# Computing what tokens read (attention weights times state) on eight array tiles with features on partitions, and loading the first weights first, in a fused attention and feed-forward kernel

## The chip, the cores and the metric

One Trainium2 chip, one of its cores. The metric is device time in microseconds (us) of one execution. A profile is one traced execution, whose span is a little shorter than the time of a run. Engines are named PE (TensorE), PEld (its weight loads), DVE (VectorE), ACT (ScalarE), POOL (GpSimd) and SP (the queue that issues most transfers).

## The reference

Eight batches of 512 tokens and 32 state rows, 8 heads of 64 features. Tokens read from the state, the state reads from the tokens, and each row of the result, normalised by its root mean square, goes through a gated feed-forward. Cut to what matters:

```python
scores = scale * np.matmul(x, state.transpose(0, 1, 3, 2))     # 512 x 32 for a head
a = softmax(scores)
xread = np.matmul(a, state)                                    # what tokens read
sread = np.matmul(softmax(scale * state @ x.T), x)             # what states read
x = concat([xread, sread]) as rows of 8 * 64 = 512 features
rms = np.sqrt(np.mean(x * x, axis=-1, keepdims=True) + 1e-06)
xn = x / rms * rms_g
out = silu(xn @ w_gate) * (xn @ w_val) @ w_out                 # 512 -> 1536 -> 512
```

All three weight matrices come as 64-bit floats. The kernel turns them into float32 itself.

## The kernel before

It never stores what tokens read. The feed-forward's first products are made as `a` times (state times weights), so `xread` is needed only for its sum of squares, from which the inverse root mean square follows. Heads lie on partitions as 4 groups `j` of 32 state rows, for `e` = 0 and 1. The old read multiplies attention weights `aT` by a block-diagonal tile `bd` of the state, tokens on partitions, and lets ACT add up the squares along the free axis:

```python
for j in range(4):                          # POOL fills the block-diagonal tile
    GE.tensor_copy(bd[Ns*j:Ns*j+Ns, :, j, :], packed[Ns*j:Ns*j+Ns])
...
ss = two.tile([P, NC], F32, name="ss")
for c in range(NC):                         # 4 chunks of 128 tokens
    rp = aps.tile([P, 2, 4 * D], F32, name="at")
    for e in range(2):
        TE.matmul(out=rp[:, e, :], lhsT=aT[:, e, c, :],
                  rhs=bd[:, e].rearrange("p j d -> p (j d)"), start=True, stop=True)   # L270
    flat = rp.rearrange("p e f -> p (e f)")
    SE.activation(out=flat, in_=flat, func=ACTF.Square, scale=DM ** -0.5,
                  accum_out=ss[:, c:c + 1])                                          # L273
    yield
rp = inverse_rms(ss, NC)                    # DVE: + 1e-6 (L174), POOL: pow -0.5 (L176),
aT_s[b] = ...                               # PE: 4 transposes (L179), DVE: scale aT (L278)
```

`attention(b + 1)` is a generator: its steps are interleaved with the feed-forward of batch b, two after each pair of hidden slices and five at each of four places of the output products. The order in which each engine's instructions stand in the trace isn't quite the source's: products are moved into gaps when the program is made (in one steady batch of the kernel before, output products run from 225.63 to 233.86 us between two groups of the read's). Batches 1 to 7 use a scheme with seven products in place of eight; its output part begins:

```python
zs = ...; product(zs, S_, TS(0), True)      # S_ = hs, sums of hidden halves, made on DVE
p5 = keep(zs)
... s = s - hb[upper] (DVE)
xs = ...; product(xs, A(0, 0), B(0, 0), True)   # needs hb alone
p1 = keep(xs)
between()                                   # five steps of attention(b + 1)
```

Weights come in 18 pieces of 1 MB. A piece is loaded raw, then ACT and DVE work on it in eight steps; the last multiplication is on DVE for the first twelve pieces and on POOL for the last six, those of `w_out`. The start is:

```python
load_x(0, nc.scalar)
load_state(0)                               # 4 small transfers
load_piece(0)
nc.sync.dma_start(out=rms_g, ...)
for k in range(1, RAW_AHEAD): load_piece(k)
for _ in attention(0): pass                 # nothing else for PE to do yet
```

Of the kernel before, what the change touches and what calls it, by code (L numbers as in the profile page):

```python
# [8 lines left out]
F32 = mybir.dt.float32  # L9
I32 = mybir.dt.int32  # L10
U32 = mybir.dt.uint32
ALU = mybir.AluOpType
ACTF = mybir.ActivationFunctionType
AXX = mybir.AxisListType.X
PSUM = bass.MemoryType.PSUM

P = 128
# [4 lines left out]
def kernel(  # L22
# [19 lines left out]
    nc = tc.nc  # L42
    VE, SE, GE, TE = nc.vector, nc.scalar, nc.gpsimd, nc.tensor

    B, H, S, D = x.shape
    Ns = state.shape[2]
    DM = H * D
    DFF = moe_w_gate.shape[1]
    NC = S // P
    NI = DM // P  # L50
    NM = DFF // P
# [5 lines left out]
    consts = ctx.enter_context(tc.tile_pool(name="consts", bufs=1))  # L57
    one = ctx.enter_context(tc.tile_pool(name="one", bufs=1))
    two = ctx.enter_context(tc.tile_pool(name="two", bufs=2))
    aps = ctx.enter_context(tc.tile_pool(name="aps", bufs=2, space=PSUM))  # L60
    vps = ctx.enter_context(tc.tile_pool(name="vps", bufs=2, space=PSUM))
# [6 lines left out]
    conv = early.enter_context(tc.tile_pool(name="conv", bufs=2))  # L68


    bds = [consts.tile([P, 2, 4, D], F32, name="bd%d" % r) for r in range(2)]
    for t in bds:
        GE.memset(t, 0.0)
    rows = {}
    x_sb = {}

    def load_state(b):

        rows[b] = two.tile([P, 2, D], F32, name="rows")
        for j in range(4):  # L80
            src = state[b, 2 * j:2 * j + 2].rearrange("e n d -> n e d")
            nc.sync.dma_start(out=rows[b][Ns * j:Ns * j + Ns], in_=src)

    def load_x(b, queue):
        x_sb[b] = one.tile([P, NC, H * D], F32, name="x_b")
        for c in range(NC):
            queue.dma_start(
                out=x_sb[b][:, c].rearrange("p (h d) -> p h d", h=H),
                in_=x[b, :, P * c:P * c + P, :].rearrange("h p d -> p h d"))
# [5 lines left out]
    ones = consts.tile([P, P], F32, name="ones")  # L95
    GE.memset(ones, 1.0)
    bounds = consts.tile([P, 2], F32, name="bounds")
# [10 lines left out]
    pieces = []  # L108
# [7 lines left out]
    raw = {}  # L116

    def load_piece(k):
        if k >= len(pieces):
            return  # L120
        dst, src = pieces[k]
        if src.dtype == F32:
            src = src.rearrange("p a (c f) -> p a c f", f=P)
            for a in range(src.shape[1]):
                nc.sync.dma_start(out=dst[:, a], in_=src[:, a])
            return
        raw[k] = raws.tile([P, 8 * P, 2], I32, name="raw")
        nc.sync.dma_start(out=raw[k].rearrange("p (a f) two -> p a (f two)", a=src.shape[1]),
                          in_=src.bitcast(I32))

    n_ready = 0

# [7 lines left out]
    def to_float32(k):  # L140


        load_piece(k + RAW_AHEAD)
        if k not in raw:
            return
        r = raw.pop(k)
        hi = r[:, :, 1]
        man = r.bitcast(F32)[:, :, 0]
        top = conv.tile([P, 8 * P], I32, name="top")
        ex = conv.tile([P, 8 * P], I32, name="ex")  # L150
        VE.tensor_scalar(ex, hi, 20, 0x7ff, op0=ALU.logical_shift_right, op1=ALU.bitwise_and)

        SE.activation(out=ex, in_=ex, func=ACTF.Relu, scale=-1.0, bias=bounds[:, 0:1])
        SE.activation(out=ex, in_=ex, func=ACTF.Relu, scale=-float(1 << 23), bias=bounds[:, 1:2])
        SE.activation(out=man, in_=r.bitcast(U32)[:, :, 0], func=ACTF.Copy, scale=2.0 ** -52)
        VE.tensor_scalar(top, hi, 0xfffff, 0x100000, op0=ALU.bitwise_and, op1=ALU.bitwise_or)
        VE.scalar_tensor_tensor(out=man, in0=top, scalar=2.0 ** -20, in1=man,
                                op0=ALU.mult, op1=ALU.add)
        VE.scalar_tensor_tensor(out=ex, in0=hi, scalar=-(1 << 31), in1=ex,
                                op0=ALU.bitwise_and, op1=ALU.bitwise_or)  # L160
        dst = pieces[k][0]
        eng = VE if k < NM else GE
        eng.tensor_tensor(out=dst, in0=man.rearrange("p (a c f) -> p a c f", f=P, c=dst.shape[2]),  # L163
                          in1=ex.bitcast(F32).rearrange("p (a c f) -> p a c f", f=P,
                                                        c=dst.shape[2]), op=ALU.mult)


    stT_g = {}
# [2 lines left out]

    def inverse_rms(ss, n):

        VE.tensor_scalar(ss, ss, 1e-6, None, op0=ALU.add)  # L174
        ri = two.tile([P, NC], F32, name="ri")
        GE.tensor_tensor(out=ri[:, 0:n], in0=ss, in1=mhalf[:, 0:n], op=ALU.pow)  # L176
        rp = aps.tile([P, NC, P], F32, name="at")
        for c in range(n):
            TE.transpose(out=rp[:, c, :], in_=ri[:, c:c + 1].to_broadcast([P, P]), identity=ident)  # L179
        return rp.rearrange("p c t -> p (c t)")  # L180

    def attention(b):
        xb, packed, bd = x_sb.pop(b), rows.pop(b), bds[b % 2]
        if b + 1 < B:
            load_state(b + 1)

# [3 lines left out]
        TE.transpose(out=tp.rearrange("p j n -> p (j n)"),  # L190
                     in_=packed.rearrange("p e d -> p (e d)"), identity=ident)
        VE.tensor_copy(stT, tp)
        for j in range(4):
            GE.tensor_copy(bd[Ns * j:Ns * j + Ns, :, j, :], packed[Ns * j:Ns * j + Ns])
        VE.tensor_tensor(out=stT_g[b], in0=stT, in1=rms_g.unsqueeze(2).to_broadcast([P, 4, Ns]),
                         op=ALU.mult)
        yield
# [10 lines left out]
        sp = [aps.tile([P, S], F32, name="at") for e in range(2)]  # L208
        for j in range(4):
            for e in range(2):  # L210
                TE.matmul(out=sp[e][Ns * j:Ns * j + Ns, :], lhsT=stT[D * e:D * e + D, j, :],  # L211
                          rhs=xT[j // 2][D * e:D * e + D, j % 2].rearrange("p c t -> p (c t)"),
                          start=True, stop=True)
        sS = one.tile([P, 2, NC, P], F32, name="sS", tag="sS")
        e2 = one.tile([P, 2, NC, P], F32, name="e2", tag="xT0")
        s2 = two.tile([P, 2], F32, name="s2")
        m2 = two.tile([P, 2], F32, name="m2")
        z2 = two.tile([P, 2], F32, name="z2")
        for e in range(2):
            SE.copy(sS[:, e].rearrange("p c t -> p (c t)"), sp[e])  # L220
            VE.reduce_max(out=m2[:, e:e + 1], in_=sS[:, e].rearrange("p c t -> p (c t)"),  # L221
                          axis=AXX)
        yield

        eS = one.tile([P, NC, 2, 4, Ns], F32, name="eS", tag="eS")
# [2 lines left out]
        for cp in range(2):  # L228
            tp = aps.tile([P, 2, 2, P], F32, name="at")
            for c in range(2):  # L230
                for e in range(2):
                    TE.transpose(out=tp[:, c, e, :], in_=sS[:, e, 2 * cp + c, :], identity=ident)
            srows = tp.rearrange("p c e (j n) -> p (c e j) n", n=Ns)
            a = eS[:, 2 * cp:2 * cp + 2].rearrange("p c e j n -> p (c e j) n")
# [3 lines left out]
                             op=ALU.subtract)  # L238
            SE.activation(out=a, in_=a, func=ACTF.Exp, scale=SCALE)
            yield  # L240

        VE.tensor_scalar(s2, m2, -SCALE, None, op0=ALU.mult)
        for e in range(2):
            SE.activation(out=e2[:, e], in_=sS[:, e], func=ACTF.Exp, scale=SCALE,  # L244
                          bias=s2[:, e:e + 1], accum_out=z2[:, e:e + 1])
        yield
        aT = one.tile([P, 2, NC, P], F32, name="aT", tag="sS")
        for cp in range(2):
            a = eS[:, 2 * cp:2 * cp + 2].rearrange("p c e j n -> p (c e j) n")
# [5 lines left out]
                             op=ALU.mult)  # L255
            tp = aps.tile([P, 2, 2, P], F32, name="at")
            for c in range(2):
                for e in range(2):
                    TE.transpose(out=tp[:, c, e, :],
                                 in_=eS[:, 2 * cp + c, e].rearrange("p j n -> p (j n)"),  # L260
# [2 lines left out]
            yield  # L263


        ss = two.tile([P, NC], F32, name="ss")
        for c in range(NC):
            rp = aps.tile([P, 2, 4 * D], F32, name="at")
            for e in range(2):
                TE.matmul(out=rp[:, e, :], lhsT=aT[:, e, c, :],  # L270
                          rhs=bd[:, e].rearrange("p j d -> p (j d)"), start=True, stop=True)
            flat = rp.rearrange("p e f -> p (e f)")
            SE.activation(out=flat, in_=flat, func=ACTF.Square, scale=DM ** -0.5,  # L273
                          accum_out=ss[:, c:c + 1])
            yield
        rp = inverse_rms(ss, NC)
        aT_s[b] = two.tile([P, 2, S], F32, name="aT_s")
        VE.tensor_tensor(out=aT_s[b], in0=aT.rearrange("p e c t -> p e (c t)"),  # L278
# [33 lines left out]
    def state_norm():  # L312

        sq = one.tile([P, NI, NT], F32, name="sqT", tag="eS")
        SE.activation(out=sq, in_=xsT, func=ACTF.Square, scale=DM ** -0.5)
        sp = aps.tile([P, NT // P], F32, name="at")
        for r in range(NT // P):
            for i in range(NI):
                TE.matmul(out=sp[:, r:r + 1], lhsT=sq[:, i, P * r:P * r + P], rhs=ones[:, 0:1],
                          start=(i == 0), stop=(i == NI - 1))  # L320
        ss = two.tile([P, NT // P], F32, name="sst")
        VE.tensor_copy(ss, sp)
        rp = inverse_rms(ss, NT // P)
        for i in range(NI):
            VE.scalar_tensor_tensor(out=xsT[:, i, :], in0=xsT[:, i, :], scalar=rms_g[:, i:i + 1],
                                    in1=rp[:, 0:NT], op0=ALU.mult, op1=ALU.mult)
        yield
# [238 lines left out]
    done = object()  # L566
    sums = iter(())
    load_x(0, nc.scalar)
    load_state(0)
    load_piece(0)  # L570
    nc.sync.dma_start(out=rms_g, in_=moe_rms_g.rearrange("(i p) -> p i", p=P))
    for k in range(1, RAW_AHEAD):
        load_piece(k)
# [79 lines left out]
```

## Time and profile before

| | before |
|---|---|
| time, median of 3 | 888.15 us (887.88 to 888.86) |
| span of the profile | 887.1 us |
| PE, DVE, ACT, POOL busy | 94, 52, 39, 21% |
| first product of the seven-product scheme | 172.5 us |
| PE idle after 199 us | 13.8 of 688 us |

The slices of the page show a head (to about 155 us), where PE often waits for DVE (12.4 us in two waits for `eS`), and a long part where PE is full. I use two marks throughout. The first is the **first product of seven**, the start of batch 1's feed-forward (batches 1 to 7 use a scheme with seven products in place of eight): from there on PE is full (busy 22.00 of the 22 us to 199 us), so the mark tells how long the head took. The second is the **period**, from that product of one batch to that of the next.

### The profile page before, as it was taken

To read this page: it belongs to the slowest core of one execution; us is meant where nothing else is said; L and a number is where in the kernel's file an instruction comes from. 1 tells how busy PE (TensorE), PEld (TensorE's weight loads), DVE (VectorE), ACT (ScalarE), POOL (GpSimd) and SP (SyncE) were. 2 spreads that over 40 slices of the span, in tenths; PEclk is the share of its full clock that TensorE was granted. 3 is DMA by queue.
4 is the path that set the end of the run, shared out by engine and by line. 5 is a ranking of instruction groups with operands and counts; after the bars stand their busy time and mean duration, and the time that the engine had idled before them with its cause. 6 is when DMAs were issued, how large, how long until landed. Compare 5 with 4: busy or idle time off the path is not lost.

```text
span 887.1 us, 11884 instructions
## 1 busy us (share of the span) xinstructions
PE 831.5 (94%) x4742; PEld 618.0 (70%) x4742; DVE 465.7 (52%) x723; ACT 346.8 (39%) x600; POOL 184.3 (21%) x255
## 2 busy tenths in 40 slices
PE   3598878999999999999999999999999999999998
PEld 1343325477787787778777777778877877788886
DVE  3889987068414762368216931585147623661131
ACT  4777753255205631364226521553056312520110
POOL 1200244132212302221222221321223022310000
PEclk9699999999999999999999999999999999999999
DMA  8465411100030003000210003000300000001000
GB/s 244 144 191 192 143 47 40 56 4 1 1 84 16 1 1 72 27 1 0 60 36 5 1 11 86 1 1 1 83 13 1 1 25 25 1 0 36 13 1 24
DMA packets 53798, 37.46 MB, mean 42 GB/s; under 512 B 37872, under 2 KB 45552, under 8 KB 53744
## 3 DMA queue, kind: packets, MB, share of 16 engines
q1 hardware_dynamic: 49584, 35.66, 13.8%
q10 hardware_dynamic: 4160, 1.05, 0.6%
q8 instruction: 37, 0.61, 0.3%
q14 instruction: 17, 0.14, 0.1%
HBM read 27.79 MB, written 8.91 MB: 41 GB/s over the span
## 4 chain that ended last, share of the span: by engine, by line
PE 69%; issue 14%; DVE 7%; POOL 4%; ACT 3%; DMA 2%; POOLq 0%; ACTq 0%; DVEq 0%
PE f L497 26%; PE f L406 22%; PE f L368 7%; PE pv L342 5%; PE f L454 2%; DMA x_b<-in_x_dram 2%; PE at L270 1%; POOL wo L163 1%; PE at L203 1%; PE at L211 1%; ACT e L244 1%; DVE m L221 1%; PE at L297 1%; POOL ri L176 1%; PE at L287 1%
## 5 line engine op out<-in xcount | busy, mean ns | idle before, releaser
L406 PE MATMUL f<-aT_s,v 128*128 128x256 f32 x504 | 131.9, 393 | 2.6 <-ACT g L423 2.6
L406 PEld LDWEIGHTS f<-aT_s,v 128*128 128x128 f32 x504 | 89.4, 189 | 52.6 <-issue 29.8
L497 PE MATMUL f<-wo,hb 128*128 128x256 f32 x540 | 124.5, 382 | 0.0
L497 PEld LDWEIGHTS f<-wo,hb 128*128 128x128 f32 x540 | 100.6, 190 | 14.5 <-ACT ot L517 0.3
L357 POOL TENSOR_TENSOR vs<-v 128x256 f32<-128x256 f32 x42 | 30.6, 729 | 320.4 <-ACT v L349 320.4
L349 ACT COPY v<-pv 128x512 f32<-128x512 f32 x96 | 51.5, 590 | 113.2 <-PE pv L342 113.0
L406 PE MATMUL f<-aT_t,vs 128*128 128x256 f32 x336 | 86.3, 379 | 0.0
L517 ACT COPY ot<-f 128x256 f32<-128x256 f32 x60 | 19.6, 375 | 170.3 <-PE f L497 170.3
L497 PE MATMUL f<-wt,hs 128*128 128x256 f32 x360 | 85.0, 380 | 0.0
L421 DVE TENSOR_TENSOR g<-g,f 128x512 f32<-128x512 f32 x42 | 28.7, 683 | 96.6 <-PE f L406 72.6
L497 PEld LDWEIGHTS f<-wt,hs 128*128 128x128 f32 x360 | 67.2, 190 | 10.4 <-DVE hs L441 1.3
L406 PEld LDWEIGHTS f<-aT_t,vs 128*128 128x128 f32 x336 | 63.8, 190 | 9.5 <-issue 0.8
L522 DVE TENSOR_TENSOR ot<-ot,f 128x256 f32<-128x256 f32 x45 | 17.1, 418 | 100.1 <-PE f L497 64.3
L342 PE MATMUL pv<-w,stT_g 64*32 64x512 f32 x768 | 60.7, 599 | 0.6 <-DVE w L163 0.6
L431 ACT ACTIVATE hb<-g 128x1024 f32<-128x1024 f32 x42 | 44.4, 1057 | 33.1 <-DVE g L425 33.1
L432 DVE SCALAR_TENSOR_TENSOR hb<-hb,g 128x1024 f32<-128x1024 f32 x42 | 51.4, 1225 | 7.0 <-ACT hb L431 7.0
L368 PE MATMUL f<-aT_s,v 128*128 128x512 f32 x96 | 45.0, 621 | 3.1 <-ACT v L349 3.1
L454 PE MATMUL f<-wo,hb 128*128 128x512 f32 x96 | 44.6, 606 | 1.1 <-DVE hb L376 1.1
L406 PE MATMUL f<-aT_t,v 128*128 128x256 f32 x168 | 43.4, 380 | 0.0
L406 PE MATMUL f<-aT_s,vs 128*128 128x256 f32 x168 | 43.1, 379 | 0.0
L368 PE MATMUL f<-xsT,w 128*128 128x256 f32 x192 | 41.6, 379 | 0.0
L425 DVE TENSOR_TENSOR g<-g,f 128x512 f32<-128x512 f32 x42 | 28.7, 684 | 24.0 <-PE f L406 23.9
(111 smaller groups left out, 1275.6 us busy)
## 6 DMA issues: line engine op xcount, KB each, us to landing
x_b<-in_x_dram SPq DMA_DIRECT2D x28, 256.0 KB, 4.5
out_dram<-ot SPq DMA_DIRECT2D x56, 128.0 KB, 1.8
raw<-in_moe_w_gate_dram SPq DMA_DIRECT2D x6, 1024.0 KB, 5.5
raw<-in_moe_w_val_dram SPq DMA_DIRECT2D x6, 1024.0 KB, 7.1
raw<-in_moe_w_out_dram SPq DMA_DIRECT2D x6, 1024.0 KB, 4.9
x_b<-in_x_dram ACTq DMA_DIRECT2D x4, 256.0 KB, 6.9
out_dram<-ot SPq DMA_DIRECT2D x4, 256.0 KB, 2.0
rows<-in_state_dram SPq DMA_DIRECT2D x32, 16.0 KB, 1.8
```

The source lines that it names most:

```text
L342: TE.matmul(out=pv[e][Ns * j:Ns * j + Ns, :], lhsT=stT_g[b][D * e:D * e + D, j, :], rhs=w[D * e:D * e + D, j, 2 * mp:2 * mp + 2].rearrange ...
L349: SE.copy(v[:, e].rearrange("p m k f -> p (m k f)"), pv[e])
L357: GE.tensor_tensor(out=vs[:, 0], in0=a21, in1=a22, op=ALU.add)
L368: TE.matmul(out=ps[:, 0:n], lhsT=lhs(i, k), rhs=r, start=(i == 0), stop=(i == len(rhs) - 1))
L406: TE.matmul(out=ps[:, i, :], lhsT=lhs[:, i, :], rhs=rhs, start=(start and i == 0), stop=True, skip_group_check=True)
L421: VE.tensor_tensor(out=g[:, :, 0, :], in0=g[:, :, 0, :], in1=ys, op=ALU.add)
L425: VE.tensor_tensor(out=g[:, :, 1, :], in0=g[:, :, 1, :], in1=zs, op=ALU.add)
L431: SE.activation(out=h, in_=gate, func=ACTF.Tanh, scale=0.5)
L432: VE.scalar_tensor_tensor(out=h, in0=h, scalar=1.0, in1=gate, op0=ALU.add, op1=ALU.mult)
L454: TE.matmul(out=op, lhsT=hb[:, m, P * r:P * r + P], rhs=wo[:, m, :], start=(m == 0), stop=(m == NM - 1))
L497: TE.matmul(out=ps[:, r, :], lhsT=lhs(k)[:, P * r:P * r + P], rhs=rhs(k), start=(start and r == 0 and k == 0), stop=(k == HM - 1), skip_gr ...
L517: SE.copy(kept[r], ps[:, r, :])
```

## The change

Intent: take PE work out of each batch. The read is made with features on partitions: 32 state rows by 64 features is one array tile, and the eight (j, e) run side by side, with 512 tokens each. Squares of the four results are added up by DVE, and a column of ones sums them over partitions. No block-diagonal tile remains. The first piece of weights comes and is converted in halves, and is issued ahead of the state rows; the maximum over tokens moves behind the token softmax. Cut to its core:

```diff
-        for j in range(4):
-            GE.tensor_copy(bd[Ns * j:Ns * j + Ns, :, j, :], packed[Ns * j:Ns * j + Ns])
@@ the read (the old loop above is removed)
+        reads = [(aps, vps)[j // 2].tile([P, S], F32, ...) for j in range(4)]
+        for j in range(4):
+            for e in range(2):
+                TE.matmul(out=reads[j][D * e:D * e + D, :],
+                          lhsT=packed[Ns * j:Ns * j + Ns, e, :],
+                          rhs=aT[Ns * j:Ns * j + Ns, e].rearrange("n c t -> n (c t)"),
+                          start=True, stop=True)
+        sq = [one.tile([P, 2, S], F32, ...) for i in range(2)]
+        for j in (2, 3, 0, 1):
+            SE.activation(out=sq[j // 2][:, j % 2, :], in_=reads[j], func=ACTF.Square,
+                          scale=DM ** -0.5)
+        yield
+        VE.tensor_tensor(out=sq[1], in0=sq[1], in1=sq[0], op=ALU.add)
+        VE.tensor_tensor(out=sq[0][:, 0, :], in0=sq[1][:, 0, :], in1=sq[1][:, 1, :], op=ALU.add)
+        sp = aps.tile([P, NC], F32, name="at")
+        for c in range(NC):
+            TE.matmul(out=sp[:, c:c + 1], lhsT=sq[0][:, 0, P * c:P * c + P], rhs=ones[:, 0:1],
+                      start=True, stop=True)
+        VE.tensor_scalar(ss, sp, 1e-6, None, op0=ALU.add)
+        yield
@@ load_piece, to_float32
+        for a in parts(k):              # two halves for piece 0, one part for all others
+            nc.sync.dma_start(out=out_[:, a], in_=src[:, a].bitcast(I32))
... (the conversion runs over the same parts)
@@ start
+    load_piece(0)
     load_state(0)
-    load_piece(0)
... (the 1e-6 moves out of inverse_rms; reduce_max over sS moves behind the exponentials)
```

More of the change, by code (lines that the diff above doesn't have):

```diff
@@ L68 @@
     conv = early.enter_context(tc.tile_pool(name="conv", bufs=2))
-    bds = [consts.tile([P, 2, 4, D], F32, name="bd%d" % r) for r in range(2)]
-    for t in bds:
-        GE.memset(t, 0.0)
     rows = {}
@@ L127, in load_piece, with parts @@
         raw[k] = raws.tile([P, 8 * P, 2], I32, name="raw")
-        nc.sync.dma_start(out=raw[k].rearrange("p (a f) two -> p a (f two)", a=src.shape[1]),
-                          in_=src.bitcast(I32))
+        out_ = raw[k].rearrange("p (a f) two -> p a (f two)", a=src.shape[1])
+        for a in parts(k):
+            nc.sync.dma_start(out=out_[:, a], in_=src[:, a].bitcast(I32))
+    def parts(k):
+        n = pieces[k][1].shape[1]
+        return (slice(0, n // 2), slice(n // 2, n)) if k == 0 else (slice(0, n),)
     n_ready = 0
@@ L145, in to_float32 @@
             return
-        r = raw.pop(k)
-        hi = r[:, :, 1]
-        man = r.bitcast(F32)[:, :, 0]
-        top = conv.tile([P, 8 * P], I32, name="top")
-        ex = conv.tile([P, 8 * P], I32, name="ex")
-        VE.tensor_scalar(ex, hi, 20, 0x7ff, op0=ALU.logical_shift_right, op1=ALU.bitwise_and)
-        SE.activation(out=ex, in_=ex, func=ACTF.Relu, scale=-1.0, bias=bounds[:, 0:1])
-        SE.activation(out=ex, in_=ex, func=ACTF.Relu, scale=-float(1 << 23), bias=bounds[:, 1:2])
-        SE.activation(out=man, in_=r.bitcast(U32)[:, :, 0], func=ACTF.Copy, scale=2.0 ** -52)
@@ L156, in to_float32 @@
-        VE.tensor_scalar(top, hi, 0xfffff, 0x100000, op0=ALU.bitwise_and, op1=ALU.bitwise_or)
-        VE.scalar_tensor_tensor(out=man, in0=top, scalar=2.0 ** -20, in1=man,
-                                op0=ALU.mult, op1=ALU.add)
-        VE.scalar_tensor_tensor(out=ex, in0=hi, scalar=-(1 << 31), in1=ex,
-                                op0=ALU.bitwise_and, op1=ALU.bitwise_or)
-        dst = pieces[k][0]
-        eng = VE if k < NM else GE
-        eng.tensor_tensor(out=dst, in0=man.rearrange("p (a c f) -> p a c f", f=P, c=dst.shape[2]),
-                          in1=ex.bitcast(F32).rearrange("p (a c f) -> p a c f", f=P,
-                                                        c=dst.shape[2]), op=ALU.mult)
+        whole = raw.pop(k)
@@ new lines, in to_float32 @@
+        tops = conv.tile([P, 8 * P], I32, name="top")
+        exs = conv.tile([P, 8 * P], I32, name="ex")
+        n = pieces[k][1].shape[1]
+        for a in parts(k):
+            cols = slice(8 * P * a.start // n, 8 * P * a.stop // n)
+            r, top, ex, dst = whole[:, cols, :], tops[:, cols], exs[:, cols], pieces[k][0][:, a]
+            hi = r[:, :, 1]
+            man = r.bitcast(F32)[:, :, 0]
+            VE.tensor_scalar(ex, hi, 20, 0x7ff, op0=ALU.logical_shift_right, op1=ALU.bitwise_and)
+            SE.activation(out=ex, in_=ex, func=ACTF.Relu, scale=-1.0, bias=bounds[:, 0:1])
+            SE.activation(out=ex, in_=ex, func=ACTF.Relu, scale=-float(1 << 23),
+                          bias=bounds[:, 1:2])
+            SE.activation(out=man, in_=r.bitcast(U32)[:, :, 0], func=ACTF.Copy, scale=2.0 ** -52)
+            VE.tensor_scalar(top, hi, 0xfffff, 0x100000, op0=ALU.bitwise_and, op1=ALU.bitwise_or)
+            VE.scalar_tensor_tensor(out=man, in0=top, scalar=2.0 ** -20, in1=man,
+                                    op0=ALU.mult, op1=ALU.add)
+            VE.scalar_tensor_tensor(out=ex, in0=hi, scalar=-(1 << 31), in1=ex,
+                                    op0=ALU.bitwise_and, op1=ALU.bitwise_or)
+            man, ex = (t.rearrange("p (a c f) -> p a c f", f=P, c=dst.shape[2])
+                       for t in (man, ex.bitcast(F32)))
+            (VE if k < NM else GE).tensor_tensor(out=dst, in0=man, in1=ex, op=ALU.mult)
@@ L172, in inverse_rms @@
     def inverse_rms(ss, n):
-        VE.tensor_scalar(ss, ss, 1e-6, None, op0=ALU.add)
         ri = two.tile([P, NC], F32, name="ri")
@@ L182, in attention @@
     def attention(b):
-        xb, packed, bd = x_sb.pop(b), rows.pop(b), bds[b % 2]
+        xb, packed = x_sb.pop(b), rows.pop(b)
         if b + 1 < B:
@@ L220, in attention @@
             SE.copy(sS[:, e].rearrange("p c t -> p (c t)"), sp[e])
-            VE.reduce_max(out=m2[:, e:e + 1], in_=sS[:, e].rearrange("p c t -> p (c t)"),
-                          axis=AXX)
         yield
@@ L240, in attention @@
             yield
+        for e in range(2):
+            VE.reduce_max(out=m2[:, e:e + 1], in_=sS[:, e].rearrange("p c t -> p (c t)"),
+                          axis=AXX)
         VE.tensor_scalar(s2, m2, -SCALE, None, op0=ALU.mult)
@@ L263, in attention @@
             yield
-        ss = two.tile([P, NC], F32, name="ss")
-        for c in range(NC):
-            rp = aps.tile([P, 2, 4 * D], F32, name="at")
-            for e in range(2):
-                TE.matmul(out=rp[:, e, :], lhsT=aT[:, e, c, :],
-                          rhs=bd[:, e].rearrange("p j d -> p (j d)"), start=True, stop=True)
-            flat = rp.rearrange("p e f -> p (e f)")
-            SE.activation(out=flat, in_=flat, func=ACTF.Square, scale=DM ** -0.5,
-                          accum_out=ss[:, c:c + 1])
-            yield
+        reads = [(aps, vps)[j // 2].tile([P, S], F32, name=("at", "pv")[j // 2]) for j in range(4)]
+        for j in range(4):
+            for e in range(2):
+                TE.matmul(out=reads[j][D * e:D * e + D, :],
+                          lhsT=packed[Ns * j:Ns * j + Ns, e, :],
+                          rhs=aT[Ns * j:Ns * j + Ns, e].rearrange("n c t -> n (c t)"),
+                          start=True, stop=True)
+        sq = [one.tile([P, 2, S], F32, name="sq%d" % i, tag=("xT1", "sq")[i]) for i in range(2)]
+        for j in (2, 3, 0, 1):
[8 more added lines that the diff above has]
+                      start=True, stop=True)
+        ss = two.tile([P, NC], F32, name="ss")
+        VE.tensor_scalar(ss, sp, 1e-6, None, op0=ALU.add)
+        yield
         rp = inverse_rms(ss, NC)
@@ L321, in state_norm @@
         ss = two.tile([P, NT // P], F32, name="sst")
-        VE.tensor_copy(ss, sp)
+        VE.tensor_scalar(ss, sp, 1e-6, None, op0=ALU.add)
         rp = inverse_rms(ss, NT // P)
```

## The prediction

The sum of the text below is 888.15 - 10.1 - 3 - 2.5 - 0.2, which came to 872.4, "say 872.5 us". Before "The change part by part" are times from the trace of the kernel before: the 16 records in 1.02 us are those of L342, its matmuls on array tiles; L319 are the one-column sums that it already has; L254 and L278 are DVE operations on two tensors.

> **What bounds the kernel now.** I began with the page: the busy shares, then the 40 slices.
>
> ```profile
> PE 831.5 (94%) x4742; PEld 618.0 (70%) x4742; DVE 465.7 (52%) x723; ACT 346.8 (39%) x600; POOL 184.3 (21%) x255
> ...
> PE   3598878999999999999999999999999999999998
> ...
> DVE  3889987068414762368216931585147623661131
> ```
>
> The reader is to see two stages. In the first seven slices of 22 us (to about 155 us) TensorE (PE) is short of work and VectorE (DVE) is full: there the 64-bit weights are turned into float32 while attention for batch 0 runs alone and that for batch 1 beside the first feed-forward. After that PE is full and no other engine is. The view of busy times by stretch puts numbers on it:
>
> ```profile
> 66.60:88.80 22.20, 18.41 (x78) 7.74 (x77) 22.20 (x29) 16.42 (x21) 0.00 (x0) 1.00 0.58 192
> 88.80:111.00 22.20, 19.42 (x58) 7.61 (x56) 22.20 (x25) 16.12 (x20) 4.93 (x2) 0.92 0.42 142
> ...
> 199.00:887.00 688.00, 674.22 (x4002) 537.44 (x3999) 326.08 (x537) 235.74 (x444) 139.53 (x199) 1.00 0.08 20
> ```
>
> Columns after the stretch: its length, then busy time of PE, weight loads, DVE, ScalarE (ACT), GpSimd (POOL), then clock, DMA share, GB/s. From 199 us on PE is busy 674.2 of 688.0 us, so only 13.8 us of it are idle. Here a microsecond less of PE work is a microsecond less of time; a microsecond on DVE (47% busy) is free unless PE waits for it. Before 155 us it is the other way round.
>
> The waits of PE after 199 us name who causes half of its idle time:
>
> ```profile
> PE at L179 <- POOL ri L176: 7.1, 7, 1.3
> ```
>
> This is the wait for the power -0.5 on POOL that ends the norm, about 1.0 us in each of seven calls. The timeline of PE shows the part that the change replaces, in one steady batch (the same pattern returns every 94.6 us):
>
> ```profile
> 224.76 1.03 PE L270 MATMUL at<-bd,aT 128*128 128x256 f32 x4
> 225.63 1.03 PE L497 MATMUL f<-wt,hs 128*128 128x256 f32 x4
> ...
> 233.86 2.99 PE L270 MATMUL at<-bd,aT 128*128 128x256 f32 x12
> 236.69 1.46 PE L497 MATMUL f<-wt,hs 128*128 128x256 f32 x6
> 239.40 0.65 PE L179 MATMUL at<-ident,ri 128*128 128x128 f32 x4 [1.25 <-POOL ri L176]
> ...
> 256.77 1.09 PE L342 MATMUL pv<-w,stT_g 64*32 64x512 f32 x16
> 257.79 5.45 PE L497 MATMUL f<-wo,hs 128*128 128x256 f32 x24
> ```
>
> I read costs here from start to start, since the printed lengths overlap their successors. Eight matmuls of L270 appear as 16 records (two to a float32 matmul): 225.63 - 224.76 = 0.87 us and 236.69 - 233.86 = 2.83 us, 3.70 us together. Eight matmuls on array tiles (L342, 64 rows by 32 columns) take 257.79 - 256.77 = 1.02 us. The order on PE isn't that of the source: other products are moved into gaps.
>
> [...]16 records in 1.02 us, though each is printed at 599 ns on the mean, so eight do run at once.[...]L319 starts 16 records from 749.21 to 750.98 us, 111 ns apart.[...] The trace has 686 ns for L254 at 512 and 1219 ns for L278 at 1024.[...] Here POOL is nearly unused where the new adds fall in the steady batches, so I count no loss there; in the head, two L156 took 3.50 us beside POOL's L163 where two alone take 1.29.
>
> **The change part by part.**
>
> *Matmuls of the read.* Removed for each batch: 3.70 us of PE. Added: eight matmuls of 32 by 64, 512 columns, estimated at L342's 1.02 us plus 0.1 us for the changes of mode (the four L406 records after an L342 take 0.97 us, others 0.87). Added: four one-column sums with 128-column weights, 8 records at 111 ns, 0.89 us. Net 3.70 - 1.12 - 0.89 = 1.69 us for a batch. Attention of batches 2 to 7 falls in the PE-bound part: 6 x 1.69 = **10.1 us**, fully on the path.
>
> *Squares.* Still four of 128x512 on ACT at about 580 ns, but without the four reads of the accumulator (194 ns each): 0.78 us less of ACT a batch, off the path.
>
> *Adds.* One of 128x1024 (1.22 us) and one of 128x512 (0.69 us): 1.9 us of DVE a batch. In steady batches DVE sits idle 5.67 us just before it makes ss at 237.67, so they fit. Their result is needed late, after the first output product, so I expect no new wait of PE.
>
> *The wait for POOL.* Before, from the end of the last L270 (236.69) to L179 (239.40) it is 2.71 us: square, accumulator read, ss, power. After, it is the sums' end, ss (0.2 us), the power (1.02 us) and some 0.3 us of signals: about 1.5 us. With the same products put into the gap the wait would fall from 1.25 to about 0.1 us; but whoever ordered them will fill the gap differently, so I count half: 0.5 us x 6 = **3 us**.
>
> *Copies into the block-diagonal tile.* 12.6 us of POOL go, and with them what stands before the power twice in the head: at 38.08 four copies of 2.52 us hold it up until 40.69 (ss was ready at 39.0: 1.7 us), and at 142.07 until 144.60 (0.9 us).
>
> *The head.* The first piece of weights arrives at 11.34 us, in one; its last two DVE steps (L159, L163, 1.23 us each) run at 18.3 to 20.8, beside attention. In halves, issued before the state rows instead of after (2.56 us), it should be converted before x is complete (15.27), which takes 2.5 us from the DVE queue; the moved maximum (L221, 1.2 us) leaves the front of the softmax. Against that: [...]two sets of adds, 3.8 us, enter a queue that is full from 44 to 117 us. The chain to the first normalised weights keeps its length otherwise: matmuls and squares get shorter, adds and sums are new (2.56 us to aT, reads 2 at the slow early clock, squares 1.7, adds 1.9, sums 1.3, ss and power 1.5, transposes 1.2: 12.2 us from L254, against 13.2). Sum: 1 to 2 us before batch 0, about 1 us around batch 1: **2.5 us**, the least certain term.
>
> *The end.* One DVE copy less in the norm of states: below 0.2 us.
>
> Sum: 888.15 - 10.1 - 3 - 2.5 - 0.2 = 872.4, say 872.5 us.
>
> **Rivals.** *A: a new wait of PE for the adds.* If sums are placed soon after reads, PE waits for four squares (2.3 us) and two adds (1.9 us), up to some 4 us a batch.[...] Against: products move across steps in the trace, and 8 us lie between the first and last L270. It would give 872.5 + 6 x 2 = 885 us or more.
>
> *B: the 32-row tiles run less than eight wide*[...]. If reads take 2 us, 6 x 0.9 us are lost: 878 us. No view before can exclude it.
>
> *C: the head takes nothing, or gives back.* DVE is full there, and 3.8 us of adds may cancel what is moved out: 875 to 877 us. The other way, earlier conversions and a freer POOL could bring 5 to 6 us: 869.
>
> *D: the wait at L179 goes wholly, or comes back fully.* 6 x 0.5 us either way: 869.5 or 875.5.
>
> **Range and chances.** The matmul saving is firm unless A or B hold; head and wait move the sum by about 4 us each way, B by 5 upward. I take 866.5 to 879.5. Faster by 2% starts at 870.7 us, only 1.8 us below the centre, so it's near a third; slower by 2% would need a wait of 5 us in each batch.
>
> **What would show it.** Matmuls from packed tiles: 16 records in about 1.0 to 1.2 us start to start (B: 2). Sums: 8 records in 0.9 us. PE busy from 199 us on lower by about 10 us. PE's wait for ri under 1 us each; a PE wait for the second add is A. The first L368, at 46.47 before, at about 45; the first L406, at 172.5 before, about 2.5 us earlier. The prediction is wrong if the period of 94.6 us falls by less than 1.2 or more than 3.2 us, or if the head moves by more than 5.

## More of the kernel before

In the kernel after, line numbers differ: L273 is the new read, L279 the squares, L282 and L283 the adds, L286 the sums, L289 `ss`, L181 the power, L184 the transposes, L421 and L512 what L406 and L497 were, L456 the sums `hs`, L171 what L163 was, and L499 the weight sums (L484).

## The result, and the profile after

The changed kernel took 882.0 us (881.47 to 882.15, 4 runs) against 888.5 of before in the same rounds. The ratio is 0.9925 (95% interval 0.9908 to 0.9942): the mean time of one kernel's fast runs over that of the other's of the same rounds, so not quite the ratio of the medians. Spans went from 887.1 to 880.3 us, 6.8 us less where 15.7 were predicted. The time lies outside the predicted range.

From the page and the view of busy times by stretch:

```profile
PE 820.6 (93%) x4806; PEld 603.9 (69%) x4806; DVE 475.8 (54%) x743; ACT 343.1 (39%) x571; POOL 168.7 (19%) x221
...
199.00:880.30 681.30, 665.79 (x4051) 526.24 (x4049) 332.90 (x548) 232.62 (x421) 131.45 (x183) 1.00 0.08 21
```

PE's busy time after 199 us fell by 674.22 - 665.79 = 8.4 us, but its idle time grew from 13.8 to 681.3 - 665.8 = 15.5 us. The waits of PE after 199 us in the changed kernel name what grew (columns: total, times, longest):

```profile
PE at L184 <- POOL ri L181: 5.2, 6, 0.9
PE f L421 <- ACT g L438: 2.9, 12, 0.3
PE f L512 <- DVE hs L456: 2.7, 6, 0.4
```

The wait for the power fell from 7.1 to 5.2 us (5.30 with a short one that this view leaves out), not by 3, and a wait that wasn't there before has come: output products wait for the sums `hs` on DVE. The timeline of PE in a steady batch of the changed kernel shows both:

```profile
226.08 0.66 PE L273 MATMUL at<-aT,rows 32*64 32x512 f32 x4
...
227.63 3.72 PE L512 MATMUL f<-wt,hs 128*128 128x256 f32 x16 [0.44 <-DVE hs L456]
231.19 4.05 PE L512 MATMUL f<-wo,hb 128*128 128x256 f32 x18
235.07 0.95 PE L286 MATMUL at<-ones,sq 128*128 128x1 f32 x8
235.88 0.68 PE L512 MATMUL f<-wo,hb 128*128 128x256 f32 x2
237.37 0.65 PE L184 MATMUL at<-ident,ri 128*128 128x128 f32 x4 [0.81 <-POOL ri L181]
```

The read ends, and 0.44 us later the next product can start. Sums end at 235.88, and transposes start 1.49 us later, just as the prediction had the chain (1.5 us); but only one matmul (2 records) stands in between, where there were three (6 records).

To account for the rest I summed for every PE record from 209.6 us (before) and 209.9 us (after), the same point of batch 1, to the end, the time from its start to the next one's start less idle time:

| six steady batches | before | after |
|---|---|---|
| old read | 22.18 us | |
| new read, sums | | 6.68 + 4.86 us |
| output products | 276.45 | 277.65 |
| state read and its transposes (L297, L287) | 12.81 | 13.42 |
| idle before L179/L184 | 7.10 | 5.30 |
| idle before hs products | 0 | 2.67 |
| other idle | 2.35 | 3.20 |

And the head: from the timelines of PE of the kernel before and of the changed kernel, the first product of seven.

```profile
172.53 1.03 PE L406 MATMUL f<-aT_s,v 128*128 128x256 f32 x4
```

```profile
172.86 1.03 PE L421 MATMUL f<-aT_s,v 128*128 128x256 f32 x4
```

It came 0.33 us later, where 2.5 us earlier was predicted. It didn't stand still, though: x and the first softmax are earlier, and the gain is lost further on. These are lines of the timelines of SP and PE of the kernel before, the issue of the second piece and the first transposes of x that didn't have to wait for x any more:

```profile
4.38 0.37 SPq L128 DMA_DIRECT2D raw<-in_moe_w_val_dram  x1
...
15.27 3.12 PE L203 MATMUL at<-ident,x_b 128*128 128x128 f32 x13 [3.37 <-DMA x_b<-in_x_dram]
```

and of the changed kernel:

```profile
9.20 0.51 SPq L127 DMA_DIRECT2D raw<-in_moe_w_val_dram  x1
...
10.64 4.00 PE L206 MATMUL at<-ident,x_b 128*128 128x128 f32 x16
```

x is complete at 11.22 instead of 15.22 us. The second megabyte of weights now starts at 9.20 instead of 4.38 us, so x shares the DMA engines with less: until x was complete, the queue of weights and state rows moved 2.99 MB in the kernel before and 1.22 MB in the changed one, beside the 1.05 MB of x. I had reckoned with the opposite, a later x, which was an estimate only. The issue of `rms_g` before it began at 8.77 us, just after x's second part had landed (8.755); what held it back wasn't tried by itself.

Then the lead goes. The first `eS` times `z` (exponentials of the token softmax times the inverse of their sum) starts at 25.4 instead of 29.0 us, yet the first normalised weights `aT_s` come at 44.14 instead of 42.92: the chain between grew from 13.9 to 18.8 us. Of these 4.9 us, 1.8 lie before the read: its first matmul comes 4.5 us after the start of `eS` (at 29.88) where it came 2.7 us after it (at 31.77), because the second half of the softmax now stands behind a conversion step in DVE's order (L167, 1.21 us at 26.16; the second `eS` starts at 27.28, 1.9 us after the first, where before the two took 1.28 us together). And a late `aT_s` alone doesn't set the end of the head: in order_only (experiment 2) it came at 44.47 us, and the first product of seven at 170.40. More is told by the first transposes of batch 1's `eS`, from the timelines of PE of the kernel before, the changed kernel and head_old_read (experiment 4, the old read in the head):

```profile
133.60 1.94 PE L259 MATMUL at<-ident,eS 128*128 128x128 f32 x8 [5.90 <-DVE eS L254]
...
131.84 1.94 PE L263 MATMUL at<-ident,eS 128*128 128x128 f32 x8 [5.89 <-DVE eS L258]
...
131.37 1.94 PE L269 MATMUL at<-ident,eS 128*128 128x128 f32 x8 [5.94 <-DVE eS L264]
```

The changed kernel still leads by 1.8 us here. From here to the first product of seven it takes 41.0 us, the kernel before 38.9 and head_old_read 38.6. So of the 2.9 us by which its head ends behind that of head_old_read, 0.5 are lost up to here and 2.4 in batch 1.

What holds it up in batch 1 is seen in these lines of the timelines of POOL, DVE and PE of the changed kernel:

```profile
137.97 2.40 POOL L171 TENSOR_TENSOR wo<-raw,ex 128x1024 f32<-128x1024 f32 x1 [7.34 <-DVE ex L167]
...
140.41 0.69 DVE L499 TENSOR_TENSOR wt<-wo 128x512 f32<-128x512 f32 x1 [2.52 <-POOL wo L171]
141.02 1.22 DVE L282 TENSOR_TENSOR sq<-sq,sq 128x1024 f32<-128x1024 f32 x1
142.16 0.68 DVE L499 TENSOR_TENSOR wt<-wo,wt 128x512 f32<-128x512 f32 x1
142.76 0.69 DVE L283 TENSOR_TENSOR sq<-sq 128x512 f32<-128x512 f32 x1
...
143.59 1.02 PE L286 MATMUL at<-ones,sq 128*128 128x1 f32 x8 [2.60 <-DVE sq L283]
```

The squares were ready at 138.6 us, but the adds stand in DVE's order behind a weight sum that waits 2.52 us for POOL's conversion of the last piece; PE idles 2.60 us for the second add. For those 2.52 us DVE stood idle and took up neither add, though the first had its squares for 1.8 of them.

PE's clock is lower too. Page, both kernels, before and after:

```profile
PEclk9699999999999999999999999999999999999999
```

```profile
PEclk9599997999999999999999999999999999999999
```

The digits are tenths of full speed. In the clock records the head of the kernel before has 27.3 us at half clock (four stretches), that of the changed one 37.5 us: 23.9 without a break from 22.6 us on, and two of 6.8, one of them from 145.5 us, 2 us after those 2.60 us of idleness. The stretches are 3.4 us or multiples of it (10.2, 6.8, 3.4 and 6.8 us before). What lowers the clock isn't shown by these runs.

The traces allow an estimate of the part that goes with the clock. The changed kernel and p1_first (experiment 8) have the same order of PE in the stretch of batch 1 above; it took 41.0 us with 10.3 us of it at half clock, and 40.0 with 7.4. combo_new_head (experiment 11) has 7.4 us at half clock as well, but the last conversion on DVE instead of POOL, and took 38.8. So about 1.0 us goes with the clock and 1.2 us with the block in DVE's order. These are traces of single executions. The total at half clock decides nothing by itself: it is 37.5 us in the head of combo_new_head and 27.3 in that of last_on_vector (experiment 6), which end at 170.76 and 170.95 us.

### The profile page after: what moved, and what is told of

It reads as the page before. It is cut to its first block, busy times and chain, and to the rows that moved or that the text cites. A ratio compares the mean times of both kernels' runs of the same rounds, so it can differ in the third digit from the quotient of the medians.

```text
span 880.3 us, 11961 instructions
## 1 busy us (share of the span) xinstructions
PE 820.6 (93%) x4806; PEld 603.9 (69%) x4806; DVE 475.8 (54%) x743; ACT 343.1 (39%) x571; POOL 168.7 (19%) x221
## 3 DMA queue, kind: packets, MB, share of 16 engines
q10 hardware_dynamic: 4160, 1.05, 0.7%
## 4 chain that ended last, share of the span: by engine, by line
PE 68%; DVE 10%; ACT 3%; issue 1%; POOL 1%; DVEq 0%; ACTq 0%
PE f L512 29%; PE f L421 23%; PE f L383 5%; PE pv L357 4%; PE f L469 2%; DVE hb L451 2%; DVE hb L447 2%; PE at L214 1%; PE at L206 1%; ACT e L248 1%; DVE hs L456 1%; DVE g L440 1%; DVE m L244 1%; PE at L302 1%; DVE hb L458 1%
## 5 line engine op out<-in xcount | busy, mean ns | idle before, releaser
L421 PE MATMUL f<-aT_s,v 128*128 128x256 f32 x504 | 131.9, 393 | 2.9 <-ACT g L438 2.9
L421 PEld LDWEIGHTS f<-aT_s,v 128*128 128x128 f32 x504 | 89.4, 189 | 52.9 <-issue 29.8
L512 PE MATMUL f<-wo,hb 128*128 128x256 f32 x540 | 122.9, 381 | 0.0
L512 PEld LDWEIGHTS f<-wo,hb 128*128 128x128 f32 x540 | 101.1, 190 | 14.9 <-ACT ot L532 1.9
L512 PE MATMUL f<-wt,hs 128*128 128x256 f32 x360 | 86.8, 383 | 2.7 <-DVE hs L456 2.7
L421 PE MATMUL f<-aT_t,vs 128*128 128x256 f32 x336 | 86.3, 379 | 0.0
L512 PEld LDWEIGHTS f<-wt,hs 128*128 128x128 f32 x360 | 65.8, 190 | 17.4 <-DVE hs L456 8.2
L421 PEld LDWEIGHTS f<-aT_t,vs 128*128 128x128 f32 x336 | 63.8, 190 | 9.5 <-issue 0.8
L383 PE MATMUL f<-aT_s,v 128*128 128x512 f32 x96 | 42.8, 599 | 2.7 <-ACT v L364 2.7
L421 PE MATMUL f<-aT_t,v 128*128 128x256 f32 x168 | 43.4, 381 | 0.0
L421 PE MATMUL f<-aT_s,vs 128*128 128x256 f32 x168 | 43.1, 379 | 0.0
L181 POOL TENSOR_TENSOR ri<-ss,mhalf 128x4 f32<-128x4 f32 x8 | 9.4, 1171 | 170.4 <-DVE ss L289 170.4
L440 DVE TENSOR_TENSOR g<-g,f 128x512 f32<-128x512 f32 x42 | 28.8, 686 | 23.9 <-PE f L421 23.9
```

The costliest lines, as they stand in the source:

```text
L383: TE.matmul(out=ps[:, 0:n], lhsT=lhs(i, k), rhs=r, start=(i == 0), stop=(i == len(rhs) - 1))
L421: TE.matmul(out=ps[:, i, :], lhsT=lhs[:, i, :], rhs=rhs, start=(start and i == 0), stop=True, skip_group_check=True)
L440: VE.tensor_tensor(out=g[:, :, 1, :], in0=g[:, :, 1, :], in1=zs, op=ALU.add)
L512: TE.matmul(out=ps[:, r, :], lhsT=lhs(k)[:, P * r:P * r + P], rhs=rhs(k), start=(start and r == 0 and k == 0), stop=(k == HM - 1), skip_gr ...
```

## The experiments

Twelve kernels ran in three sets of four (1, 3, 4, 5; then 6, 7, 8, 10; then 2, 9, 11, 12 by the numbers below), each beside the kernel before on the same chip; the medians of before in the sets were 890.38, 890.03 and 889.82 us. Runs of the kernel before spread from 887.7 to 893.1, wider than the first measurement, so I read the marks in the traces first and the times second. A mark comes from one trace for each run. The changed kernel, after_again and p1_first, whose heads are the same, agree within 0.1 us (172.77 to 172.86); the kernel before and before_p1 differ by 1.1 us (172.53 and 173.65), as x was complete at 15.22 and at 16.27. So with the old order of loads a mark is good to about a microsecond. Theory: in the head, the adds and sums lengthen a chain that the old read had spread out, and eat what the early loads give; in steady batches, PE gets to its next products before DVE and POOL are ready, because the order of products is unlucky. Rivals: the head can't be shortened at all (DVE full); the row tiles are slow; the waits would only move.

### 1. The loads alone: loads_only

The kernel before with the load part of the change only:

```diff
+    load_piece(0)        # in halves, converted in halves
     load_state(0)
-    load_piece(0)
```

> The kernel before with nothing of the change but the first piece loaded and converted in halves and issued ahead of the state rows. Theory (the head's gain is real, and is eaten later by the adds of the read): x lands near 11.2 us as in the changed kernel instead of 15.2, the first normalised exponentials (eS times z) are done about 3.5 us earlier than the 29.1 us of before, the whole run is 2 to 4 us faster than before (884.5 to 886.5), with the first product of seven (172.5 us before) 2 us or more earlier. Rival (a full VectorE queue swallows any early gain whatever the read does): within 0.7 us of before, first product of seven at 172 to 173.

Measured: x lands at 11.18 us, first product of seven at 169.37 (3.2 us earlier than before), 887.88 us, ratio 0.9966 (0.9947 to 0.9984). The head gain is real and not swallowed by a full DVE queue: the rival falls. The first softmax was less early than expected (27.2 us, not 25.6). The time gained only 0.3%; in the profile the last stretch lost 1.6 us, and the view of busy times by stretch says where (clock is the third column from the end), before first, then loads_only:

```profile
737.00:760.00 23.00, 22.74 (x133) 17.04 (x131) 10.15 (x17) 9.55 (x16) 6.37 (x9) 1.00 0.05 18
```

```profile
737.00:760.00 23.00, 22.74 (x134) 15.55 (x133) 11.14 (x18) 9.54 (x16) 6.34 (x9) 0.93 0.04 12
```

PE fell to half clock for 3.4 us, from 750.0 on, as in read_only below but in no other trace here. Such dips don't explain the spread of times by themselves: in the second set, four runs of the kernel before with a mean clock of 0.983 took 888.37 to 891.55 us.

### 2. Order without halves: order_only

The kernel before with `load_piece(0)` ahead of `load_state(0)`, the piece whole.

> The kernel before with one pair of lines swapped: the first piece of weights, whole, is issued ahead of the state rows. It tells the order of loads from the halves. If the early x is a matter of order (the second piece is issued at 9.2 us instead of 4.4, so x has the DMA engines more to itself): x lands before 12 us, and first product of seven comes at 169.4 to 170.5, nearly as with order and halves (169.4). If it takes the halves: x at 14 us or later, 171.5 to 172.8.

x at 11.46 us, first product of seven at 170.40, 887.17 us, ratio 0.9971 (0.9953 to 0.9989). So by these traces 2.1 of the 3.2 us are the order of two lines, and 1.0 us is the halves; the scatter told above is as large as the second.

### 3. The read alone: read_only

The changed kernel with loads as before.

> The changed kernel with the loads put back as before: one piece, behind the state rows. Theory: the adds lengthen the chain of batch 0 by about 4 us and hold up batch 1 by 2 us, and no early x pays for it, so first product of seven at 174 to 176 us (172.5 before, 172.9 changed), time 883.5 to 885.5 (882.0 changed). Rival: the head ends where it did, at 172.5 to 173, time 882.

First product of seven at 176.94 us, 887.64 us, ratio 0.996 (0.9939 to 0.9982). The mark moved as the theory said, a little more: the read costs the head 4.4 us against before. The loads are worth 176.94 - 172.86 = 4.1 us beside it. But x was complete at 16.64 us in this trace; against before_p1 (16.27 us) the read costs 3.3 us, so about 1 us of both figures can be x. Unlike in the changed kernel, most of the loss lies in batch 0: batch 1's transposes start 2.75 us later than in before_p1 (137.48 and 134.73), and the stretch after them takes 39.5 us against 38.9. The time was 2 us higher than expected; 1.7 of them in the profile are the end after the last period (148.4 us against 146.7), where the dip at 750 us told above lies.

### 4. The old read in the head: head_old_read

```diff
+        if b < 2:
+            ... block-diagonal tile, matmuls and accumulated squares as before ...
+        else:
             reads = ...
```

> The changed kernel, but batches 0 and 1, whose attention lies in the head, read by the old block-diagonal matmuls with squares added up by ScalarE; no adds there. Theory (adds wait in VectorE's order behind conversion work and weight sums, and PE for them: 1.85 and 2.60 us): no such PE wait, first product of seven 2 to 3 us earlier than 172.9, time 879 to 880.5. Rival (something else holds the head's end, such as conversion of the last words on GpSimd): 881.5 to 882.5.

First product of seven at 169.96 us, 2.9 us earlier than in the changed kernel; 878.08 us, ratio 0.986 (0.9838 to 0.9882), faster even than expected. DVE is held up by POOL here too, but nothing except `ss` stands behind it, as two lines of DVE's timeline of this run show:

```profile
139.93 1.29 DVE L517 TENSOR_TENSOR wt<-wo 128x512 f32<-128x512 f32 x2 [2.52 <-POOL wo L172]
141.15 0.16 DVE L287 TENSOR_SCALAR ss<-ss 128x4 f32<-128x4 f32 x1
```

`ss` is started at 141.15 us against 144.65 in the changed kernel: ACT had added up the squares meanwhile.

### 5. Sums on PE in the head: head_pe_sums

The changed kernel, but for b < 2 no adds; PE sums all four squares.

```diff
-        VE.tensor_tensor(...)  # both adds, for b < 2
+                TE.matmul(out=sp[:, c:c + 1], lhsT=term[:, P * c:P * c + P], rhs=ones[:, 0:1],
+                          start=(i == 0), stop=(i == len(terms) - 1))   # 4 terms
```

> The changed kernel, but in batches 0 and 1 the two adds are left out and TensorE adds up all four squares: 16 one-column matmuls in four groups instead of 4, which costs PE 24 more records of about 110 ns (2.6 us a batch) where it has idle time. Theory: the two PE waits for the second add go, batch 0 gains 2 to 4 us in its chain, first product of seven 1.5 to 3 us earlier, time 879 to 880.5. Rival: PE's extra 2.6 us a batch and the conversion work eat it, 881.5 to 883.

A miss. First product of seven at 178.41 us, 5.6 later than in the changed kernel, 889.94 us, ratio 0.9986 (0.9965 to 1.0006). From the timelines of PE and DVE of this run:

```profile
36.95 6.56 PE L291 MATMUL at<-ones,sq 128*128 128x1 f32 x30
```

```profile
43.54 0.16 DVE L294 TENSOR_SCALAR ss<-at 128x4 f32<-128x4 f32 x1 [7.59 <-PE at L291]
```

A one-column record takes about 216 ns here (6.48 us for 30), not the 111 I had counted with (in the changed kernel's trace they start 213 ns apart at 38.85 us, at half clock, and 112 at 235.07, at full), and `ss` holds DVE idle for 7.59 us while words wait to be converted. So leaving out the adds doesn't help when what replaces them is longer: the length of the chain from read to `ss` counts, whichever engine has it: what came next in DVE's order, the word conversion L171, started at 43.62 us, behind `ss`. What the adds alone cost isn't separated by this run.

### 6. The last conversion on DVE: last_on_vector

```diff
-            (VE if k < NM else GE).tensor_tensor(out=dst, in0=man, in1=ex, op=ALU.mult)
+            (VE if k < NM or k == len(pieces) - 1 else GE).tensor_tensor(...)
```

> The changed kernel; only the final product of the last piece of weights moves from GpSimd (2.40 us) to VectorE (about 1.2 us). Order of all PE work is unchanged. Theory (the adds of batch 1 stand in VectorE's order behind the first weight sum, which waits 2.52 us for that product): the second add ends about 1 us or more earlier, PE's wait for it (2.60 us) falls below 1.5, first product of seven 1 to 2.5 us earlier than 172.9, time 0.7 to 2.5 us less than the changed kernel. Rival (weight sums' whole length on VectorE or the clock sets the head's end): no change, within 0.5 us.

First product of seven at 170.95 us, 1.9 earlier than in the changed kernel run beside it (172.81); 880.08 us against 882.39, ratio to before 0.9896 (0.9875 to 0.9917). DVE's wait for POOL is gone, but PE's wait for the second add only fell from 2.60 to 1.79 us, not below 1.5. Half-clock time in the head fell from 37.5 to 27.3 us, so a part of the gain can go with the clock; combo_new_head, with the same head and 37.5 us, ended it at 170.76 all the same. So the block in DVE's order is one cause, and by the estimate above about half of the loss in batch 1.

### 7. The changed kernel again: after_again

> The changed kernel once more, beside the others on one chip: 0.990 to 0.994 of before, period of a steady batch 93.28 us, first product of seven at 172.9 us.

882.39 us, ratio 0.9913 (0.9895 to 0.9931), first product of seven at 172.81, periods 93.26 to 93.27 (after 94.35 for the first).

### 8. Another product first: p1_first

```diff
+        xs = fx.tile([P, 2, HD], F32, name="f")
+        product(xs, A(0, 0), B(0, 0), True)
+        p1 = keep(xs)
         zs = fz.tile([P, 2, HD], F32, name="f")
         product(zs, S_, TS(0), True)
         p5 = keep(zs)
         ...
-        xs = fx.tile(...); product(xs, A(0, 0), B(0, 0), True); p1 = keep(xs)
```

> The changed kernel, but in the output products the one that needs no sums of hidden halves is put first, so that PE has it to do while VectorE finishes the sums hs. Theory (0.44 us of a steady batch is PE waiting for hs, and 0.8 us for the power because only one product stands between sums and transposes; here three do): no wait for hs, the wait for ri under 0.3 us, period 93.28 falls to 92.0 to 92.4, total 5 to 7 us less than the changed kernel. Rival (the waits move to other places[...]): period 93.0 or more.

873.99 us, ratio 0.9821 (0.9801 to 0.9841), period 91.89 (one of 92.23): 1.4 us less than the changed kernel's, slightly more than expected. The timeline of PE:

```profile
229.28 5.34 PE L512 MATMUL f<-wt,hs 128*128 128x256 f32 x24
234.46 0.95 PE L286 MATMUL at<-ones,sq 128*128 128x1 f32 x8
235.27 1.54 PE L512 MATMUL f<-wt,hs 128*128 128x256 f32 x6
236.84 0.65 PE L184 MATMUL at<-ident,ri 128*128 128x128 f32 x4
```

No wait for `hs` in the first line; and with three matmuls (6 records) instead of one between sums and transposes, none for the power. In all six batches one wait for the power is left, of 0.4 us, in the period of 92.23. Otherwise both waits went, and didn't come back elsewhere.

### 9. The same swap without the change: before_p1

> The kernel before with the same swap as p1_first: the output product that needs no hidden sums goes first. A control: is the swap worth something without the change? In the kernel before, PE already has three products between the last read and the transposes, and no wait for hs. Theory: nothing to gain; wait for ri stays near 1.25 us, period 94.2 to 94.6, time within 0.5 per cent of before. Rival (the swap is good by itself and p1_first owes its gain to it alone): period 93.2 or less, 5 us or more faster than before.

889.55 us, ratio 0.9987 (0.9969 to 1.0005), periods 94.22 to 94.56 after the first. The waits of PE after 199 us are as in the kernel before:

```profile
PE at L179 <- POOL ri L176: 7.1, 7, 1.3
```

The swap is worth nothing by itself. It lets the change's own saving through: 94.2 to 94.6 without the change, 91.9 with it.

### 10. The read twice: double_read

```diff
-        for j in range(4):
+        for j in [0, 1, 2, 3] * 2:
```

> The changed kernel with the eight read matmuls issued twice to the same place (same result), in otherwise the same order of PE: the read's cost measured by itself. If eight tiles of 32 by 64 run side by side and the PE wait for hs that follows (0.44 us) is set by VectorE, the period grows by 1.0 minus 0.44, to 93.8 to 93.95. If the wait is unrelated, by 1.0 to 1.1, to 94.3 or more. If row tiles do not run side by side, by 2 or more. The head grows by 1 to 3 us too, where the clock is at half.

The period is 93.61 us, 0.33 more and less than expected; 888.43 us in all, much of that from the head (first product of seven at 176.2). The second set of eight matmuls costs 1.90 - 1.11 = 0.79 us on PE, not 1.0, and the 0.44 us wait for `hs` is gone from the list of waits: 0.79 - 0.44 = 0.35. So eight tiles do run side by side (rival B falls), and in the changed kernel the read sits before a point where DVE sets the pace, so that part of what it saves there is idle time.

### 11 and 12. Together: combo_new_head, combo_old_head

p1_first with last_on_vector, first with the new read everywhere, then with the old read in batches 0 and 1.

> The changed kernel with p1_first and last_on_vector together. If the two gains add up: period 91.9, first product of seven at 171 us, ratio to before 0.979 to 0.981, about 2 us faster than p1_first alone.

> The changed kernel with p1_first, last_on_vector and the old read in batches 0 and 1. If the gains add up: first product of seven at 168.5 to 170 us, period 91.9, ratio to before 0.976 to 0.979, the fastest of all. If last_on_vector and head_old_read remove the same wait twice, within 0.7 us of the better of both, 169.5 to 170.5.

| | time | ratio to before | first product of seven | period |
|---|---|---|---|---|
| combo_new_head | 872.10 us | 0.9798 (0.9779 to 0.9816) | 170.76 us | 91.91 us |
| combo_old_head | 868.78 us | 0.976 (0.9741 to 0.9779) | 166.97 us | 91.91 us, one of 92.27 |

The gains add up, in the second kernel by more than I expected. combo_old_head beats both kernels, the one before by 2.4%, the changed one by some 1.5% (0.976 over the 0.9913 of after_again).

All kernels were correct. Not tried: the moved maximum by itself, and the queue of conversion work apart from PE's half clock. They weren't told apart: for batch 1 there is the estimate from single traces above, for batch 0 none.

## Why the prediction was wrong, point by point

- **Matmuls of the read: right.** Predicted 1.69 us a batch, 10.1 in all. Read and sums took 11.54 where the old read took 22.18: 10.6. What was missed is what surrounds them: output products and the state read in the changed order cost 1.20 + 0.61 = 1.8 us more over six batches. A part is seen: the first record behind the read took 320 ns and the one behind the sums 299, where most others took 216. The rest wasn't traced. The net is 8.8 us.
- **The wait for POOL: right chain, wrong use of it.** The chain is 1.49 us, as predicted. The gap it leaves was filled with one matmul instead of three, so the wait fell from 7.10 to 5.30 us: 1.8 instead of 3. That this is a matter of order alone, p1_first shows.
- **"So they fit": the step that failed in the steady batches.** The adds themselves fit, with no PE wait for them (rival A fell there; it came true in the head). But "I expect no new wait of PE" was wrong. The shorter read brings PE to the products of `hs` 0.44 us before DVE has them: 2.67 us in six batches, plus 0.85 of smaller waits. I had looked at what the change's own results are needed for, and not at what PE would do next when it came there sooner.
- **The head: the other step that failed.** Predicted 2.5 us earlier, measured 0.3 later. Both of its terms were mis-sized. The loads give 3.2 us alone and 4.1 beside the new read (I allowed 1 to 2). The read I took to shorten the chain by 1.0 us; it costs the head 2.9 us against the old read with the new loads, and 4.4 against before (3.3 against before_p1). I added durations of steps as if each found its engine free; in batch 0 the chain from the first `eS` to `aT_s` took 18.8 us where 13.9 were before. Rival C was the right one here, but its reason, DVE's load of adds, isn't the whole: with the same adds and the last conversion on DVE the head ended 1.9 us earlier (last_on_vector). What the runs show is the adds' place in the order of a busy DVE (2.52 us behind a weight sum in batch 1); time of PE at half clock goes with it (10.3 us in the changed kernel's stretch of batch 1, 3.3 in that of before).
- **POOL's copies.** They did go, but not their delay: the power in batch 0 took 1.86 us instead of 1.03, and ended at 42.93 us instead of 41.72. A DVE instruction with two inputs (L167, 1.22 us at 40.83) ran beside it for 0.98 us, where DVE had stood idle beside the power of before; that the one slowed the other wasn't tried by itself. What had been won in POOL's queue was lost upstream. The prediction counted no such loss in the steady batches, which was right (a power took 1.02 us there, beside an idle DVE); its example from the head, two L156 beside L163, is the opposite case, a longer time of DVE beside POOL.
- **Sum.** Read and neighbours -8.8, waits +1.7 (-1.8 + 2.67 + 0.85), head +0.3: -6.8 us, which is the difference of the spans. Against the prediction's sum the waits are off by 4.7 us, the head by 2.8 and the matmuls by 1.3.

## What to carry to other kernels

When work is taken from the bounding engine, list what that engine meets next and when the others have it ready; the saved time turns into waiting there unless independent work is put first, and here one swap of two products, worthless before the change, was worth 1.4 us in each batch after it. In a head where several engines are nearly full, don't add up durations: an instruction that joins a busy engine's order waits behind what stands there (here the adds, behind a weight sum that itself waited 2.52 us), so a shorter operation with a later start can be the longer chain (18.8 us from `eS` to `aT_s` against 13.9). Use different versions for the head and for the steady part when different engines bound them.
